# Ranked heads from tile 1 on, fp16 loads over GpSimd's ring, and reordering on VectorE, in a fused attention and MoE kernel

## The chip, the cores and the metric

The kernel runs on one core of one Trainium2 chip. The metric is the device time of one execution in microseconds. The kernel before takes 238.72 us (median of 3 runs, 238.43 to 239.06). The engines are TensorE (PE in the profile; PEld is its weight load), VectorE (DVE), ScalarE (ACT), GpSimd (POOL) and SyncE (SP), which here only issues DMAs.

## The reference

The input is causal attention over 4 batches, 8 heads, 768 positions and head size 64, followed by a MoE-like layer. Three of the eight heads ("retrieval") attend to all earlier positions; the others see 4 sink positions and a window of 64.

```python
scores = q @ k.T / sqrt(64)
mask   = causal if is_retrieval[h] else causal & (is_sink | in_window)
x      = softmax(where(mask, scores, -1e9)) @ v     # -> [3072, 512]
h      = x @ w_in                                   # w_in  [512, 2048]
out    = (h - tanh(h)) @ w_out                      # w_out [2048, 512]
```

## The kernel before

The work goes by tiles of 256 positions: 12 tiles, three to a batch. The attention of a tile is woven into the MoE matmuls of the tile before, so that TensorE always has something to do. A small planner written in Python orders the operations of each engine; a tile of MoE work is eight units, about 2.1 us each.

From tile 3 on the heads are handled "by rank": the position of each head among the retrieval and the other heads is held in registers, and streaming heads take a cheaper near path. The kernel before brings q, k and v as fp32 over SyncE's queue, and GpSimd copies each head to its rank and makes fp16 of it:

```python
def ranked(t):
    return first and fast and t >= NG          # NG = 3 tiles per batch
...
def cast_ranked(t):
    for half in range(2):
        for nm in ("qk", "v"):
            for rank in range(half * HH, half * HH + HH):
                at = bass.ds(regs["POOL"][rank], 1)
                ...
                nc.gpsimd.tensor_copy(
                    out=t16[t % 2][:, :, :, rank : rank + 1, :],
                    in_=raws["rqk", t][0]()[:, :, :, at, :],
                )
    for i in range(NB):                        # then q and k are transposed by DMA
        nc.sync.dma_start_transpose(out=qk[...], in_=t16[t % 2][:, i]...)
```

The attention output of a ranked tile (`x16t`) is also transposed by DMA into `xT`, which the first MoE matmuls (`ph`) of the next stretch need:

```python
def st_X_tile(t):
    for i in range(NB):
        nc.sync.dma_start_transpose(
            out=xTs[t]()[:, :, i * 128 : i * 128 + 128],
            in_=x16s[t]()[:, i, :, :].rearrange("p h d -> p (h d)"),
        )
```

How early a tile's attention is done before its MoE work is one constant, in units:

```python
AHEAD = 2.0
ahead = (AHEAD if t > NG else 0.0, AHEAD) if ranked(t) else (0.0, 0.0)
SPAN[t] = (lo + cut[t % NG] - ahead[0], lo + cut[t % NG + 1] - ahead[1])
```

The softmax here doesn't subtract the row's maximum and nothing guards it: scores larger than these inputs give would overflow.

Of the kernel before, what the change touches and what calls it, by code (L numbers as in the profile page):

```python
# [16 lines left out]
class Plan:  # L17
# [16 lines left out]
    def op(self, eng, ns, fn, r=(), w=(), dma=None, prio=None, port=False, after=None, behind=None):  # L34
        i = len(self.ops)
        deps = set() if after is None else {after}
        for k in r:
            if k in self.writer:
                deps.add(self.writer[k])
            if k[0] in self.PSUM:  # L40
                deps.update(j for j in self.readers.get(k, ()) if self.ops[j][0] != eng)
            self.readers.setdefault(k, []).append(i)
# [16 lines left out]
    def run(self):  # L59
# [45 lines left out]
        while len(order) < n:  # L105
# [28 lines left out]
            _, ns, _, _, dma, _, port, _ = self.ops[i]  # L134
            self.start[i] = t
# [4 lines left out]
            for u in followers[i]:  # L140
                ready[u] = max(ready[u], t + ns)
                left[u] -= 1
                if not left[u]:
                    enqueue(u)
            if dma:
                packets, each = dma
                rings["POOL" if e == "POOL" else "SP"].append(
                    [i, t + ns + (1200 if e == "POOL" else 300), each, packets * each / 16]
                )
            else:  # L150
                finish(i, t + ns + self.RESULT[e])
# [6 lines left out]
def kernel(  # L158
# [64 lines left out]
    gate = const.tile([1, 1], FP16, name="gate")  # L223
    A4 = const.tile([128, 4, 128], FP16, name="A4")
    sinks = const.tile([128, 128], FP16, name="sinks")
    nz = const.tile([128, 2 * H], FP32, name="nz")
# [30 lines left out]
    def program(first):  # L257

        P = Plan(bufs)
        op = P.op  # L260
        rot = {}
# [26 lines left out]
        def paired(nm, t):  # L288

            return nm != "v" and t == 0  # L290

        def load(t, names="qkv", halves=(None,), blocks=range(NB), after=None):

            b, g = divmod(t, NG)
            for half in halves:
                h0, nh = (0, H) if half is None else (half * HH, HH)
                for nm in names:
                    src = {"q": q, "k": k, "v": v}[nm]
                    tag = "rv" if nm == "v" else "rqk"
                    if (tag, t) not in raws:  # L300
                        idx = rot[tag] = rot.get(tag, -1) + 1
                        shape = [128, NB, H, D] if nm == "v" else [128, NB, 2, H, D]
                        raws[tag, t] = (
                            lazy(raw_pool, shape, FP32, tag, f"raw_{tag}{t}"), idx
                        )
                    if paired(nm, t):
                        op(
                            "SP", max(420, 128 * nh * 1.1),
                            lambda nm=nm, src=src, h0=h0, nh=nh: nc.sync.dma_start(
                                out=raw_pairs(nm, t)[:, h0 : h0 + nh, :, :].rearrange(  # L310
                                    "p h e d -> p h (e d)"
                                ),
                                in_=src[b, h0 : h0 + nh, g * TT : (g + 1) * TT, :].rearrange(
                                    "h (p e) d -> p h (e d)", e=NB
                                ),
                            ),
                            w=[
                                key for x in (range(2) if half is None else (half,))
                                for key in raw_keys(nm, t, x)
                            ],  # L320
                            dma=(128 * nh, 26.0), after=after,
                        )
                        continue
                    for i in blocks:
                        s0 = g * TT + i * 128
                        op(
                            "SP", max(420, 128 * nh * 1.1),
                            lambda nm=nm, i=i, src=src, s0=s0, h0=h0, nh=nh: nc.sync.dma_start(
                                out=raw_of(nm, t)[:, i, h0 : h0 + nh, :],
                                in_=src[b, h0 : h0 + nh, s0 : s0 + 128, :].rearrange("h p d -> p h d"),  # L330
                            ),
                            w=[
                                key for x in (range(2) if half is None else (half,))
                                for key in raw_keys(nm, t, x, (i,))
                            ],
                            dma=(128 * nh, 18.3), after=after,
                        )

        def raw_pairs(nm, t):
            r = raws["rqk", t][0]()  # L340
            return r[:].rearrange("p i x h d -> p (i x h d)").rearrange(
# [3 lines left out]
        def raw_of(nm, t):  # L345
            if paired(nm, t):
                return raw_pairs(nm, t).rearrange("p h e d -> p e h d")
            r = raws["rv" if nm == "v" else "rqk", t][0]()
            return r[:] if nm == "v" else r[:, :, "qk".index(nm), :, :]

        def raw_keys(nm, t, half, blocks=range(NB)):
            tag = "rv" if nm == "v" else "rqk"
            return [(tag, raws[tag, t][1], nm, half, i) for i in blocks]
# [11 lines left out]
        def load_cast(t, w_after=(), names="qkv"):  # L365

            b, g = divmod(t, NG)
            for nm in names:
# [21 lines left out]
                for i in range(NB):  # L390
                    behind(
                        930, lambda fn=fn, i=i: fn((i,)), r=w_after,
                        w=[key for half in range(2) for key in t16_keys(nm, t, half, (i,))],
                        dma=(128 * H, 18.5),
                    )

# [25 lines left out]


# [8 lines left out]
        for half in range(2):  # L432
            load(0, "qk", (half,))
            load(0, "v", (half,))
        if first:

            op("POOL", 204, lambda: nc.gpsimd.memset(ones[:], 1.0), w=["ones"])
# [6 lines left out]
            if fast:  # L444
# [10 lines left out]
            def select(m, src, fill, base, step, mult, key, cmp=ALU.is_ge):  # L455
# [8 lines left out]


            select(ident16[:], ones[:], 0.0, 0, 1, -1, "ident", ALU.is_equal)
            select(A4[:, 2, :], ones[:], 0.5, window_i - 1, -1, 1, "A4")
            select(sinks[:], ones[:], 0.5, n_sink_i - 1, 0, -1, "sinks")
            op(
                "DVE", 220,  # L470
                lambda: nc.vector.tensor_max(out=A4[:, 0, :], in0=A4[:, 2, :], in1=sinks[:]),
                r=["A4", "sinks"], w=["A40"],
            )
            select(A4[:, 2, :], A4[:, 2, :], 0.0, 0, 1, -1, "A4")
            select(A4[:, 3, :], ones[:], 0.5, -(128 - window_i + 1), -1, 1, "A43")
            op(
                "DVE", 220,
                lambda: nc.vector.tensor_max(out=A4[:, 1, :], in0=A4[:, 3, :], in1=sinks[:]),
                r=["A43", "sinks"], w=["A41"],
            )  # L480
            select(A4[:, 0, :], A4[:, 0, :], 0.0, 0, 1, -1, "A40")
            if fast:
                select(mS[0:64, 3, :], ones[0:64, :], 0.0, window_i - 65, -1, 1, "mS3")
                select(mS[64:128, 3, :], ones[64:128, :], 0.0, n_sink_i - 1, 0, -1, "mS3")

# [19 lines left out]
            def make_rflag0():  # L505

                nc.vector.scalar_tensor_tensor(
                    out=rflag0[:], in0=sinks[:, 0:1].to_broadcast([128, H]), scalar=0.75,
# [3 lines left out]
            op("DVE", 165, make_rflag0, r=["sinks", "rflag"], w=["rflag0"])  # L512

# [20 lines left out]
        def ranked(t):  # L534
            return first and fast and t >= NG

        def by_rank(after):

            def dve(ns, fn, r, w):
                op("DVE", ns, fn, r=r, w=w, after=after)  # L540
# [54 lines left out]
            )  # L595
            dve(
# [15 lines left out]
                    out=rflagr0[:], in0=sinks[:, 0:1].to_broadcast([128, NGEN]), scalar=0.75,  # L612
# [10 lines left out]
                r=["A4", "A40", "A41", "A43"], w=["mS"], port=True, after=after,  # L623
# [4 lines left out]
                r=["mS3"], w=["mS"], port=True, after=after,  # L628
            )
            for e, et in (("POOL", Engine.Pool), ("DVE", Engine.DVE)):  # L630

                def get(e=e, et=et):
                    regs[e] = nc.values_load_multi_w_load_instructions(
                        perm_i[0:1, :], engines=[et], min_val=0, max_val=H - 1,
                        skip_runtime_bounds_check_because="each head has one rank below H",
                    )[1]

                op(e, 900, get, r=["perm"], w=["regs" + e])
# [9 lines left out]
        def t16_keys(nm, t, half, blocks=range(NB)):  # L648
            return [("t16", t % 2, nm, half, i) for i in blocks]

        def cast_qk(t, engines, halves=range(2)):

            for half in halves:
                for nm, es in zip("qk", engines):
                    hs = slice(half * HH, half * HH + HH)
                    cast_op(
                        es[half], NB * HH * D,
                        lambda nm=nm, hs=hs: t16[t % 2][:, :, "qk".index(nm), hs, :],
                        lambda nm=nm, hs=hs: raw_of(nm, t)[:, :, hs, :],
                        r=raw_keys(nm, t, half), w=t16_keys(nm, t, half),  # L660
                    )

        def cast_ranked(t):
            b, g = divmod(t, NG)
            lo = g * NB
            if b not in v1s:
                ones_v(b)
            for half in range(2):
                for nm in ("qk", "v"):
                    for rank in range(half * HH, half * HH + HH):  # L670

# [771 lines left out]
```

## Time and profile before

| | before |
|---|---|
| time, median | 238.72 us |
| TensorE busy | 94% of the span |
| VectorE, GpSimd busy | 59%, 38% |
| first `ph` matmul | 18.93 us |
| last matmul ends | 231.81 us |
| TensorE work by weights | 205.2 us, so 26.6 us idle before the last matmul |

The work by weights counts each matmul at the distance at which the same kind follows itself undisturbed (109 ns for 256 columns, and so on; the prediction tells how). "Idle" below always means time up to the last matmul less this work.

The columns of these lines are packets, megabytes, and the time that the packets took as a share of the span of the 16 DMA engines; packets overlap, so the shares can add up to more than 100%. The last line is from another part of the page: issues, kilobytes of each, median us from issue to landing.

```profile
q1 hardware_dynamic: 92642, 28.98, 60.5%
q0 software_dynamic: 15168, 5.77, 20.7%
...
raw_rqk<-in_q_dram SPq DMA_DIRECT2D x20, 256.0 KB, 4.7
```

q1 is SyncE's queue, q0 is GpSimd's ring.

### The profile page before, as it was taken

The page shows a single profiled execution, that of the slowest core. Times are in us where ns is not written, and L with a number is a line of the kernel's source. Part 1 is how long each engine was busy: PE and PEld are TensorE (multiplying, and loading weights), DVE is VectorE, ACT ScalarE, POOL GpSimd, SP SyncE. Part 2 cuts the span into 40 slices and gives each one's busy share as a digit, 9 for nine tenths or more (in the row PEclk, how much of TensorE's full clock was granted, in tenths as well). Part 3 has the DMA queues.
Part 4 walks back from the last instruction along what each step waited for, and adds up shares of the span by engine and source line. Part 5 has one row for each costly group of instructions (what it writes and reads, how often), then busy time and mean ns, then how long its engine had stood idle before and what let it go on. Part 6 is the DMA issues. An engine that isn't in the chain of part 4 may idle for free. (4 is left out here: it accounts for less than half of the span.)

```text
span 236.7 us, 5895 instructions
## 1 busy us (share of the span) xinstructions
PE 221.5 (94%) x2220; PEld 157.8 (67%) x2220; DVE 139.0 (59%) x343; ACT 143.6 (61%) x221; POOL 90.5 (38%) x218
## 2 busy tenths in 40 slices
PE   0889899999999999999999999999999999999991
PEld 0346687756776777777676777776776777777661
DVE  1856665864488657767666655667766546443300
ACT  3668677884588387466686649537759464444320
POOL 5999420089818068480814904606300000000000
PEclk9999999999999999999999999999999999999999
DMA  5999999999997999979989695998712101310121
GB/s 128 209 140 172 204 181 204 197 228 224 206 225 182 151 248 184 227 153 206 239 168 214 136 186 130 186 171 179 134 47 66 38 31 47 90 38 9 44 89 51
DMA packets 108130, 35.29 MB, mean 149 GB/s; under 512 B 100290, under 2 KB 104642, under 8 KB 108098
## 3 DMA queue, kind: packets, MB, share of 16 engines
q1 hardware_dynamic: 92642, 28.98, 60.5%
q0 software_dynamic: 15168, 5.77, 20.7%
q8 instruction: 18, 0.29, 0.5%
q10 hardware_dynamic: 288, 0.14, 0.2%
q14 instruction: 14, 0.11, 0.2%
HBM read 27.27 MB, written 6.29 MB: 142 GB/s over the span
## 5 line engine op out<-in xcount | busy, mean ns | idle before, releaser
L1135 PE MATMUL ph<-xT,win 128*128 128x256 f16 x768 | 101.7, 273 | 0.6 <-DMA win<-in_moe_w_in_dram 0.3
L1194 PE MATMUL po<-wout,gt 128*128 128x512 f16 (+1 forms) x400 | 98.0, 371 | 0.3 <-ACT ot L1170 0.3
L1148 ACT ACTIVATE th<-ph 128x512 f32<-128x512 f32 x96 | 57.6, 601 | 59.6 <-PE ph L1135 58.2
L1155 DVE SCALAR_TENSOR_TENSOR gt<-th,ph 128x512 f16<-128x512 f32 x96 | 65.4, 684 | 44.9 <-ACT th L1148 44.4
L1135 PEld LDWEIGHTS <-win 128*128 128x128 f16 x768 | 80.0, 114 | 13.0 <-issue 1.9
L961 ACT ACTIVATE pt<-sc 128x1024 f16<-128x1024 f32 (+1 forms) x78 | 68.5, 926 | 11.4 <-PE sc L941 10.9
L1194 PEld LDWEIGHTS <-gt 128*128 128x128 f16 x400 | 36.4, 98 | 24.6 <-issue 0.9
L680 POOL CAST t<-raw_rqk 128x256 f16 x72 | 28.5, 440 | 63.3 <-DMA raw_rqk<-in_k_dram 48.1
L1030 PEld LDWEIGHTS <-pt 128*128 128x128 f16 x552 | 25.9, 98 | 10.4 <-issue 0.9
L1030 PE MATMUL av<-v,pt 128*128 128x65 f16 x304 | 26.0, 195 | 0.1
L941 PE MATMUL sc<-qk 64*128 64x128 f16 (+1 forms) x412 | 23.8, 240 | 1.7 <-DVE qk L826 1.7
L941 PEld LDWEIGHTS <-qk 64*128 64x128 f16 x412 | 13.7, 94 | 13.5 <-issue 8.9
L675 POOL CAST v<-raw_rv 128x128 f16 x72 | 21.1, 335 | 4.2 <-DMA raw_rv<-in_v_dram 4.2
L1060 DVE TENSOR_TENSOR x16t<-av,rinv 128x128 f32 x72 | 20.8, 289 | 2.3 <-DVE rinv L1050 0.3
L1030 PE MATMUL av<-vf,pt 128*128 128x65 f16 x248 | 19.6, 193 | 0.0
L1170 ACT ACTIVATE ot<-po 128x512 f32<-128x512 f32 (+1 forms) x24 | 14.3, 596 | 8.5 <-PE po L1194 8.4
L996 DVE TENSOR_TENSOR pt<-pt,m 128x1024 f16<-128x1024 f16 x16 | 12.3, 768 | 8.0 <-ACT pt L961 8.0
L1050 DVE RECIPROCAL rinv<-av 128x4 f32<-128x4 f32 x48 | 8.6, 179 | 13.4 <-PE av L1030 13.4
L986 DVE TENSOR_TENSOR pt<-pt,mS 128x512 f16<-128x512 f16 x24 | 9.8, 449 | 6.7 <-ACT pt L961 6.7
L843 PEld LDWEIGHTS <-t 128*128 128x128 f16 x48 | 3.9, 107 | 8.9 <-ACT t L644 6.8
L523 DVE TENSOR_SCALAR m<-A,thr 128x512 f16<-128x512 f16 x16 | 7.4, 501 | 1.7 <-PE sc L928 1.2
L751 POOL TENSOR_TENSOR vf<-v,rflagr 128x260 f16<-128x260 f16 x12 | 7.5, 634 | 0.0
(95 smaller groups left out, 90.8 us busy)
## 6 DMA issues: line engine op xcount, KB each, us to landing
out_dram<-ot SPq DMA_DIRECT2D x23, 256.0 KB, 2.3
raw_rqk<-in_q_dram SPq DMA_DIRECT2D x20, 256.0 KB, 4.7
raw_rqk<-in_k_dram SPq DMA_DIRECT2D x20, 256.0 KB, 4.5
raw_rv<-in_v_dram SPq DMA_DIRECT2D x18, 256.0 KB, 4.4
win<-in_moe_w_in_dram POOLq DMA_DIRECT2D x4, 512.0 KB, 8.8
wout<-in_moe_w_out_dram POOLq DMA_DIRECT2D x4, 512.0 KB, 12.4
raw_rv<-in_v_dram SPq DMA_DIRECT2D x4, 128.0 KB, 4.7
t<-in_q_dram POOLq DMA_DIRECT2D x4, 128.0 KB, 9.5
```

The source lines that it names most:

```text
L675: nc.gpsimd.tensor_copy(out=v1s[b]()[:, lo : lo + NB, rank : rank + 1, 0:D], in_=raw_of("v", t)[:, :, at, :],)
L680: nc.gpsimd.tensor_copy(out=t16[t % 2][:, :, :, rank : rank + 1, :], in_=raws["rqk", t][0]()[:, :, :, at, :],)
L941: nc.tensor.matmul(out=sc()[:, hh, o : o + nb * 128].rearrange("p (i c) -> p i c", c=128), lhsT=ks.rearrange("p i c -> p (i c)")[p_, jb * ...
L961: lambda pt=pt, gi=gi, wid=wid, sc=sc: nc.scalar.activation(out=pt()[:, :, 512 * gi : 512 * gi + wid], in_=sc()[:, :, 0:wid], func=AF.Exp, ...
L996: nc.vector.tensor_mul(out=pv, in0=pv, in1=m4[:, h0 : h0 + 2, 256:512].unsqueeze(2).to_broadcast([128, 2, 2, 256]),)
L1030: nc.tensor.matmul(out=av()[:, i, hh, :], lhsT=pt()[:, hh, co : co + 128], rhs=vv, start=(jb == first_jb), stop=(jb == qb),)
L1060: nc.vector.tensor_mul(out=x16s[t]()[:, :, at, :], in0=av()[:, :, hh : hh + 1, 0:D], in1=rinv()[:, :, hh : hh + 1].unsqueeze(3).to_broadca ...
L1135: nc.tensor.matmul(out=ph()[:, j, :], lhsT=w()[:, cb, c0 + fb % 4 : c0 + 512 : 4], rhs=xTs[t]()[:, cb, :], start=(cb == 0), stop=(cb == HP ...
L1148: lambda: nc.scalar.activation(out=th()[:], in_=ph()[:], func=AF.Tanh, scale=1.0 / XS),
L1155: lambda: nc.vector.scalar_tensor_tensor(out=gts[t]()[:, u * FU : (u + 1) * FU, :], in0=th()[:], scalar=-XS, in1=ph()[:], op0=ALU.mult, op ...
L1170: nc.scalar.activation(out=ot()[:, c0:c1], in_=po()[:, c0:c1], func=AF.Copy, scale=1.0 / XS)
L1194: nc.tensor.matmul(out=po()[:, c0:c1], lhsT=gts[t]()[:, f, ts * 128 : ts * 128 + 128], rhs=w_out_t[f // 4]()[:, f % 4, c0:c1], start=(f == ...
```

## The change

The intent: (1) handle batch 0 by rank from tile 1 on, so that TensorE loses mask matmuls, scores and attention matmuls; (2) bring q, k and v as fp16, converted by the DMA itself on GpSimd's ring, in the order of heads (all but k of tile 0); (3) let VectorE put the heads in the order of ranks, from fp16 to fp16, so that GpSimd has no casts left. The core of the diff, cut:

```diff
         def ranked(t):
-            return first and fast and t >= NG
+            return by_ranks and t > 0
...
+        def load_flight(t, nm, pairs=range(HP), blocks=range(NB), after=None):
+            ...
+            for i in blocks:
+                behind(
+                    200 + 128 * nh * 0.72,
+                    lambda i=i, s0=s0: nc.gpsimd.dma_start(       # fp32 in memory -> fp16 in SBUF
+                        out=raw_of(nm, t)[:, i, h0 : h0 + nh, :],
+                        in_=src[b, h0 : h0 + nh, s0 : s0 + 128, :].rearrange("h p d -> p h d"),
+                    ), ...
+                )
...
         def cast_ranked(t):
-                            at = bass.ds(regs["POOL"][rank], 1)
-                                nc.gpsimd.tensor_copy(
+            es = ('DVE',) if t == 1 else ('DVE',) if t == 2 else ('DVE',)
+                        cast_rank(t, nm, rank, es[rank % len(es)])
...
-            ahead = (AHEAD if t > NG else 0.0, AHEAD) if ranked(t) else (0.0, 0.0)
+            ahead = (AHEAD, AHEAD) if ranked(t) else (0.0, 0.0)
```

The rest rewrites the start: q and v of tile 0 are loaded over the ring, its k still as fp32 over SyncE's queue, the rank arithmetic comes first, the masks are made on VectorE, tiles 1 and 2 are transposed by TensorE and tile 1's x as well.

## The prediction

> **What bounds the kernel now.** I read the page first, for the busy shares.
>
> ```profile
> span 236.7 us, 5895 instructions
> PE 221.5 (94%) x2220; PEld 157.8 (67%) x2220; DVE 139.0 (59%) x343; ACT 143.6 (61%) x221; POOL 90.5 (38%) x218
> PE   0889899999999999999999999999999999999991
> DVE  1856665864488657767666655667766546443300
> POOL 5999420089818068480814904606300000000000
> ```
>
> TensorE is busy from slice 2 to the end; nothing else comes near. VectorE and GpSimd have room on average. Next the waits of TensorE.
>
> ```profile
> PE tp0q L843 <- ACT t L644: 6.0, 1, 6.0
> PE sc L941 <- DVE qk L826: 1.7, 3, 0.7
> PE xp L1108 <- DVE x L1074: 1.1, 3, 0.6
> ```
>
> After the first 6.0 us the recorded waits are about 5 us in all. That flatters the kernel, because "busy" covers the latency of a matmul. So I took the distance between the starts of consecutive matmuls from the trace (median): 109 ns for 256 columns, 216 for 512, 29 for a 65-column attention-times-v, 56 for a 128-column transpose. Score matmuls use half of the rows and two run side by side: 28 for 128 columns, 56 for 256. These weights times the counts give 205.2 us of TensorE work. The last matmul ends at 231.8, so 26.6 us are idle by this measure. The timeline tells where:
>
> ```profile
> 6.00 0.39 PE L843 MATMUL tp0q<-ident,t 128*128 128x128 f16 x2 [6.00 <-ACT t L644]
> ...
> 18.93 1.06 PE L1135 MATMUL ph<-xT,win 128*128 128x256 f16 x8
> ```
>
> Until the first MoE matmul at 18.93 only 5.5 us of work are done: 13.5 us idle in the start-up of tile 0, a chain of short operations over four engines. From 18.9 to 60 us another 5 us or so are idle, and from 60 us on only 0.3 to 0.6 us per 10 us. So there are two places to gain: less TensorE work, worth its full size after 60 us, and a shorter start-up. Relief for GpSimd by itself is worth nothing.
>
> ```profile
> L680 POOL CAST t<-raw_rqk 128x256 f16 x72 | 28.5, 440 | 63.3 <-DMA raw_rqk<-in_k_dram 48.1
> L675 POOL CAST v<-raw_rv 128x128 f16 x72 | 21.1, 335 | 4.2 <-DMA raw_rv<-in_v_dram 4.2
> L1155 DVE SCALAR_TENSOR_TENSOR gt<-th,ph 128x512 f16<-128x512 f32 x96 | 65.4, 684 | 44.9 <-ACT th L1148 44.4
> L928 PE MATMUL sc<-m,ident 128*128 128x512 f16 x8 | 2.5, 400 | 0.0
> ```
>
> The first two groups are the copies by rank that go from GpSimd to VectorE; the third is what VectorE must not delay, as it frees the bank that the next MoE matmuls write; the fourth disappears.
>
> **What the Trainium skill says.** "DMA: Bandwidth & Descriptors", section "SWDGE vs HWDGE vs iDMA": a DMA that changes the type must be issued from GpSimd, whose cores write the descriptors into rings in SBUF. The trace agrees that GpSimd pays for it: the 12 such issues for q, k, v took 0.87 to 1.10 us each. "SBUF — State Buffer", section "Who interferes with whom": a VectorE copy in a two-port mode and GpSimd hold a shared port exclusively, and the later one blocks. The trace agrees:
>
> ```profile
> 5.82 1.73 DVE L523 TENSOR_SCALAR m<-A,thr 128x512 f16<-128x512 f16 x4 [0.44 <-POOL A L458]
> ...
> 6.09 1.98 POOL L378 DMA_DIRECT2D t<-in_q_dram  x2
> ```
>
> Four mask operations beside two DMA issues took 1.73 us; the third of them alone is 815 ns in the trace, until its DMA issue was over, while the undisturbed ones are 335 ns. "VectorE: DVE Perf Modes", section "What auto-detection actually checks": copies of 16-bit data within SBUF take the fastest mode. Here the one such copy (128x128) took 184 ns, and the next operation started 119 ns after it. So a copy by rank should fall from GpSimd's 440 and 335 ns to about 0.17 us (256 elements) and 0.12 us (128) of VectorE's queue, an estimate. The register operation in front of each runs ahead in the sequencer (57 ns).
>
> **The change, part by part.** The order of instructions of both kernels gives exact counts for the path that runs.
> 1. Tiles 1 and 2 by rank, half of their heads with the near path. Mask matmuls 8 x 512 columns go: 8 x 216 ns = 1.7 us. Scores: 24 fewer of 256 columns, 8 more of 128: 24 x 56 - 8 x 28 = 1.1 us. Attention-times-v: 552 to 512, 40 x 29 ns = 1.2 us. Transposes: 8 more for k of tile 0 (once by head, again by rank), 8 fewer for x of tile 2, which goes by DMA: zero. Total 4.0 us less TensorE work, 201.2 us. Of it about 0.4 us lay before 18.9 us.
> 2. GpSimd: 144 casts (50 us) go; 66 DMA issues of 0.93 us (61 us) plus four half ones come instead of 12. It stays at some 40% and off the path. SP loses its loads. Bytes read from memory are the same; the written ones halve. In steady state the loads are two tiles ahead, and six issues are 5.6 us of a tile's 17 us: hidden.
> 3. VectorE: 88 qk copies and 88 v copies plus 16 for tile 0: 88 x 0.17 + 104 x 0.12 = 27 us, some 2.5 us per tile. Without overlaps it now spends about 10 us of a 17 us tile (8 x 0.60 for gt, 8 x 0.28 for x, four masks 2.8, reciprocals 0.4), so it goes from 60% to 75%. TensorE has two banks for ph, so a delay of about 2 us is hidden. I allow 1 us of new waits in all.
> 4. Start-up. ACT loses casts (three of 0.62 us become two), and the masks come from VectorE before the data lands. But the rank arithmetic, which lay at 41 to 46 us beside MoE work, moves into the first 13 us, with the register load (845 ns in the trace), four more masks, 16 copies, four more strided copies of k (0.34) and the xT copies that ACT did (0.2). The first MoE matmul needs the fourth xT, and before it VectorE's order has, from 5.15 us when thr is ready: 12 masks at 0.42, as disturbed as now (5.0); 20 small operations (2.2); the load (0.85); eight strided copies at 0.34 (2.7); x and reciprocals (2.0); xT and tr10 (1.0); 16 copies of tile 0 (1.9); eight of tile 1 (1.4). Together 17.1, so the first ph at about 22 us if nothing overlaps, and 20.0 if the masks are undisturbed (0.26). I take 21.2, that is 2.3 us later than 18.93.
>
> **The sum.** Before: 18.93 + 199.75 us of remaining work + 13.1 idle = 231.8. After: 5.1 us of work lie before the first ph, 196.1 remain. 21.2 + 196.1 + 13.1 + 1.0 = 231.4; the tail to the end of the span is 4.9 and the measured time is 2.0 above the span: 238.3. Against this stands that the idle time between 18.9 and 60 us (5 us) should shrink: tile 1 has no mask matmuls in front of its scores and fewer exponentials (ACT's count falls by two of 1.02 us and four of 0.81 us), GpSimd no longer makes 1.07 us products that block VectorE's masks, and its SBUF-reading casts are gone, which brings pt masks from 768 to about 690 ns. I give that 2.0 us: 236.3 us.
>
> **Rivals.** (a) The start-up is not delayed: transposes and ACT, not VectorE, set it, and q arrives without a cast; then the whole 4.0 us and the 2.0 us show: about 233 us. For it: VectorE had 2.2 us busy of the 5 us from 10 to 15 us. Against: 17 us of work stand in its queue now. (b) VectorE becomes the bound in tile 0's MoE phase: 14.7 us of its work (eight gt, masks, x, copies for tiles 1 and 2) face about 12.4 us of TensorE work there. Then another 2 to 3 us are lost and it is 239 to 241 us. (c) Descriptor writing and fast copies block each other in every tile: 16 copies per tile, a fifth of them held 0.3 us is 1 us of VectorE per tile, hidden at 75%; if it is 3 us per tile, the occupancy passes 90% and TensorE waits: 242 us and more. (d) The single ring delivers too late: a landing took 4 to 5 us quiet and up to 13.7 us behind weights. Tile 2 sits between weights on the ring, so a wait at 35 to 45 us is possible: 1 to 3 us.
>
> **Range and chances.** 236.3 us, a little below the before. (a) gives the low end near 232, (b) and (d) the high end near 240.5. Faster by over 2% means under 233.9: 0.27, since it needs the start-up to cost nothing. Slower by over 2% means over 243.5: 0.04, needing (c).
>
> **What would show it.** Step 1: the counts of matmuls above, and TensorE from 60 us to the end as dense as now. Step 2: no casts on GpSimd, about 70 issues near 0.93 us. Step 3: copies of 150 to 250 ns with means raised by collisions, VectorE near 70% busy. Step 4: the first ph matmul at 20 to 22 us. I am wrong if it comes at or before 19 us, if TensorE waits for gt by more than a few us in the later tiles, or if the copies take over 300 ns.

## More of the kernel before

The view of the tile xT ends with the time from issue to landing of the DMA transposes of x:

```profile
DMA to landing us min/median/max: 2.3/2.8/4.7
```

## The result, and the profile after

The changed kernel takes 255.2 us (median of 4 runs, 251.41 to 255.41) against 238.8 us for the kernel before in the same rounds. Ratios here are the mean time of one kernel's fast runs over that of the other's of the same rounds, so they are not quite the ratio of the medians quoted. Executions over 1.5% slower than the fastest of the same kernel are left out of the means. The ratio is 1.0605, with a 95% interval of 1.0474 to 1.0737: slower by 6%. Two of its four runs (255.38 and 255.41) differ by only 0.1% from the profiled one (255.03); the other run is 251.41. So the changed kernel itself scatters by 4 us, where the kernel before scattered by 0.6 in these rounds.

The page of the changed kernel, busy shares and slices:

```profile
span 253.3 us, 5884 instructions
...
PE 224.8 (89%) x2156; PEld 157.7 (62%) x2156; DVE 164.8 (65%) x552; ACT 135.9 (54%) x209; POOL 93.8 (37%) x132
...
PE   0868989798889999995999999993999999999992
...
DVE  6999688484988876864668747754577555543410
...
PEclk9999999999999999998899999999799999999998
```

Against the rows of before: TensorE was 9 or 8 throughout. Now there are two holes, a 5 and a 3, in slices 19 and 28 (a slice is 6.3 us), and the row of the granted clock dips at or just after them. VectorE is at 65%, so it is not full. The waits of TensorE (total us, times, longest):

```profile
PE ph L1409 <- DMA xT<-x16t: 7.6, 2, 4.4
PE sc L1172 <- DVE m L706: 5.9, 2, 5.5
PE xp L1382 <- DVE x L1324: 2.0, 1, 2.0
PE av L1275 <- POOL vf L981: 1.5, 1, 1.5
```

The first line did not exist before. The first MoE matmuls of two tiles wait for the DMA transpose of x. The timeline shows the end of the start-up, and the first of the two waits:

```profile
22.05 2.77 PE L1409 MATMUL ph<-xT,win 128*128 128x256 f16 x12
...
114.85 0.34 PE L1275 MATMUL av<-v,pt 128*128 128x65 f16 x6
118.35 2.55 PE L1409 MATMUL ph<-xT,win 128*128 128x256 f16 x12 [3.15 <-DMA xT<-x16t]
```

And SyncE's part of the same timeline, the two transposes that were waited for:

```profile
109.77 2.56 SPq L1362 DMA_TRANSPOSE xT<-x16t  x2
```

They were issued at 109.77 and 111.05 us. TensorE ran out of other work at 115.19. By the trace's records they landed at 116.04 and 118.30, that is after 6.3 and 7.2 us. With the 2.8 us that such a transpose took in the median before, the second would have landed at 113.85 and nothing would have waited. At the second place (tile 8) they took 7.9 and 8.6 us. Over the whole kernel the view of xT says:

```profile
DMA to landing us min/median/max: 2.4/3.9/8.6
```

What shares the DMA engines with them is in the queue table and among the issues:

```profile
q0 software_dynamic: 75520, 13.37, 72.6%
q1 hardware_dynamic: 34400, 14.03, 28.2%
...
raw_rqk<-in_q_dram POOLq DMA_DIRECT2D x22, 128.0 KB, 6.0
```

All loads of q, k and v moved from q1 to q0, except that of tile 0's k. They write half the bytes, yet a load lands in 6.0 us, not 4.7. The packets fit this: in the trace a converting packet (128 bytes written) took 32 ns in the median in both kernels, a plain 256-byte packet of SyncE's loads 18 ns. The number of packets per load is the same, so by these medians the load holds the engines longer although it writes less. The kernel before already had 12,288 of the converting packets, so this could be read there.

The wait brings a second loss. In windows of 1 us (columns: window, length, busy time and instructions of PE, PEld, DVE, ACT and POOL, then the granted clock, the DMA share, GB/s):

```profile
117.00:118.00 1.00, 0.00 (x0) 0.00 (x0) 0.21 (x2) 0.00 (x0) 0.00 (x0) 1.00 3.10 146
118.00:119.00 1.00, 0.65 (x5) 0.53 (x6) 1.00 (x6) 0.00 (x0) 0.00 (x0) 0.81 3.20 150
119.00:120.00 1.00, 1.00 (x6) 0.74 (x5) 0.56 (x5) 0.00 (x0) 0.00 (x0) 0.50 2.74 173
...
121.00:122.00 1.00, 1.00 (x5) 0.41 (x4) 0.67 (x3) 0.00 (x0) 0.00 (x0) 0.50 0.00 0
122.00:123.00 1.00, 1.00 (x12) 0.62 (x12) 0.37 (x2) 0.00 (x0) 0.00 (x0) 0.99 0.09 18
```

After the wait TensorE ran at half its clock for over 3 us: 5 or 6 matmuls per us, then 12. The Trainium skill's page "TensorE: Matmul & The Clock Gate", section "What's actually happening", describes this: the clock is throttled to one half after an idle window of some 3.4 us and released after a busy one. The trace agrees in kind and in the length of the slow stretch: its clock records give one half from 118.62 to 122.03 us, and again from 176.6 to 180 us after the second wait. The idle time before the first was a little shorter than the page's window, 3.15 us, and other runs had the half clock after still shorter gaps (last section).

The start hides the same loss. In the timeline above, the twelve `ph` matmuls from 22.05 us took 2.77 us; at 109 ns each and the latency of the last they should take about half of that. From there up to 26.46 us matmuls of one kind follow each other at twice their normal distance. The trace has no clock record before 26.46 us, and the first one says full clock; the PEclk row prints 9 also where there is no record. So TensorE still ran at half clock there: from 22.05 to 26.46 us it did 2.25 us of work by weights, and lost 2.2 us. In the kernel before, the first record of full clock is at 14.95 us, ahead of its first `ph`. In all twelve profiled runs with the new start-up TensorE was at half clock until 23.6 to 26.6 us; five of them have it in their records, beginning at 16.7 to 18.0 us. In the four runs with the old start-up it was at full clock from 16.0 us at the latest. One of the five, e_start, shows the dip in its row:

```profile
PEclk9986999799999999999799999999799999999999
```

The share of each part in the 16.5 us by which the last matmul ends later (248.28 less 231.81), with idle as defined above:

| | before | after | difference |
|---|---|---|---|
| TensorE work | 205.2 | 201.2 | -4.0 |
| idle, 0 to 40 us | 17.1 | 22.6 | +5.4 |
| idle, 40 to 80 us | 3.9 | 6.6 | +2.6 |
| idle, 80 us to the last matmul | 5.5 | 18.0 | +12.4 |

The 4.0 us that the change was made for are there. Of the 20.4 us that ate them, 12.4 are after 80 us, where before only 5.5 were idle. They hold 7.6 us of waits for xT, and 3.3 us that the slow matmuls after these waits took beyond their normal distance (1.7 at 115 to 125 us, 1.6 at 175 to 185 us). The two make 10.9 of the 12.4 us. The 5.4 us before 40 us are 3.4 before the first `ph` and 2.0 after it (from 3.65 to 5.64 us), and these 2.0 are the half clock up to 26.46 us.

### The profile page after: what moved, and what is told of

It is laid out like the page before. It is cut to its first block, busy times and chain, and to the rows that moved or that the text cites. A ratio compares the mean times of both kernels' runs of the same rounds, so it can differ in the third digit from the quotient of the medians.

```text
span 253.3 us, 5884 instructions
## 1 busy us (share of the span) xinstructions
PE 224.8 (89%) x2156; PEld 157.7 (62%) x2156; DVE 164.8 (65%) x552; ACT 135.9 (54%) x209; POOL 93.8 (37%) x132
## 5 line engine op out<-in xcount | busy, mean ns | idle before, releaser
L1409 PE MATMUL ph<-xT,win 128*128 128x256 f16 x768 | 105.5, 279 | 9.1 <-DMA xT<-x16t 7.6
L1205 ACT ACTIVATE pt<-sc 128x1024 f16<-128x1024 f32 (+1 forms) x72 | 63.3, 930 | 19.8 <-PE sc L1185 19.7
L1275 PEld LDWEIGHTS <-pt 128*128 128x128 f16 x512 | 25.1, 100 | 15.2 <-issue 4.7
L961 POOL TENSOR_TENSOR vf<-v,rflagr 128x260 f16<-128x260 f16 x16 | 10.7, 684 | 44.3 <-DVE v L1026 44.2
L1310 DVE TENSOR_TENSOR x16t<-av,rinv 128x128 f32 x88 | 25.3, 288 | 2.2 <-DVE rinv L1300 0.4
L433 POOL DMA_DIRECT2D raw_rqk<-in_q_dram x26 | 22.9, 889 | 5.4 <-DVE qk L1026 2.7
L1185 PE MATMUL sc<-qk 64*128 64x128 f16 (+1 forms) x396 | 22.2, 242 | 1.5 <-DMA qk<-t 1.0
L1275 PE MATMUL av<-vf,pt 128*128 128x65 f16 x224 | 18.7, 193 | 2.8 <-POOL vf L981 1.5
L1185 PEld LDWEIGHTS <-qk 64*128 64x128 f16 x396 | 13.3, 96 | 11.7 <-issue 9.9
L433 POOL DMA_DIRECT2D raw_rqk<-in_k_dram x22 | 19.6, 897 | 1.6 <-DMA wout<-in_moe_w_out_dram 1.6
L433 POOL DMA_DIRECT2D raw_rv<-in_v_dram x22 | 19.5, 901 | 1.5 <-DMA wout<-in_moe_w_out_dram 1.5
L1026 DVE COPY t<-raw_rqk 128x256 f16 x88 | 15.2, 244 | 7.3 <-DMA raw_rqk<-in_k_dram 5.1
L981 POOL COPY vf<-v 64x260 f16<-64x260 f16 (+1 forms) x12 | 5.9, 489 | 34.7 <-DVE v L1026 34.3
L1300 DVE RECIPROCAL rinv<-av 128x4 f32<-128x4 f32 x48 | 8.5, 177 | 13.4 <-PE av L1275 13.2
L1230 DVE TENSOR_TENSOR pt<-pt,mS 128x512 f16<-128x512 f16 x32 | 12.1, 418 | 7.4 <-ACT pt L1205 7.4
```

Source lines behind the costliest of these rows:

```text
L433: lambda i=i, s0=s0: nc.gpsimd.dma_start(out=raw_of(nm, t)[:, i, h0 : h0 + nh, :], in_=src[b, h0 : h0 + nh, s0 : s0 + 128, :].rearrange("h ...
L1026: engs[e].tensor_copy(out=dst, in_=src)
L1185: nc.tensor.matmul(out=sc()[:, hh, o : o + nb * 128].rearrange("p (i c) -> p i c", c=128), lhsT=ks.rearrange("p i c -> p (i c)")[p_, jb * ...
L1205: lambda pt=pt, gi=gi, wid=wid, sc=sc: nc.scalar.activation(out=pt()[:, :, 512 * gi : 512 * gi + wid], in_=sc()[:, :, 0:wid], func=AF.Exp, ...
L1230: nc.vector.tensor_mul(out=pv, in0=pv, in1=m[:, 384:640].unsqueeze(1).to_broadcast([128, 2, 256]),)
L1275: nc.tensor.matmul(out=av()[:, i, hh, :], lhsT=pt()[:, hh, co : co + 128], rhs=vv, start=(jb == first_jb), stop=(jb == qb),)
```

## The experiments

Fourteen kernels ran, all with correct results; medians of before in their rounds were 238.4 to 239.0. The main theory, called R (for ring): loads on the ring lengthen the DMA transposes of x, and the slack of two units is then too small. The rivals: VectorE is too loaded with the copies (V; the first expectations call it D), and the start-up and tiles 1 and 2 by rank are what costs (S). The table is for reference; "changed" and "before" name the kernel edited.

| run | edited | median us | ratio | idle 0-40 / 40-80 / 80-end | waits for xT |
|---|---|---|---|---|---|
| kernel before | | 238.8 | 1 | 17.1 / 3.9 / 5.5 | 0 |
| changed kernel | | 255.2 | 1.0605 | 22.6 / 6.6 / 18.0 | 7.6 |
| e_sp_pool | changed | 257.4 | 1.0741 | 25.8 / 15.9 / 7.4 | 0 |
| e_sp_dve | changed | 264.0 | 1.1023 | 26.5 / 16.9 / 11.7 | 2.0 |
| e_ring_only | before | 248.9 | 1.0386 | 17.1 / 6.1 / 10.7 | 2.9 |
| e_xt_pe | changed | 249.1 | 1.0385 | 23.2 / 5.9 / 9.0 | 0 |
| e_sp_gated | changed | 249.6 | 1.0422 | 22.8 / 4.9 / 13.2 | 3.7 |
| e_ring_pool | before | 243.5 | 1.0159 | 17.1 / 6.7 / 7.3 | 2.4 |
| e_ahead4 | changed | 244.4 | 1.0177 | 22.8 / 6.9 / 6.8 | 0 |
| e_start | changed | 258.5 | 1.0751 | 22.1 / 9.5 / 18.7 | 8.4 |
| e_before_ahead4 | before | 240.6 | 1.0075 | 17.1 / 3.9 / 7.3 | 0 |
| e_gated_ahead4 | changed | 245.9 | 1.0281 | 22.8 / 4.7 / 9.8 | 0 |
| e_pool_ahead4 | changed | 244.5 | 1.0197 | 22.8 / 6.4 / 10.5 (slow run) | 0.2 |
| e_v_act | changed | 246.2 | 1.0338 | 24.1 / 5.3 / 7.0 | 0 |
| e_vf_act | changed | 245.9 | 1.0203 | 24.3 / 7.5 / 7.2 (slow run) | 0 |
| e_both_act | changed | 241.9 | 1.0110 | 21.8 / 5.4 / 7.1 | 0 |

The idle columns are of the one profiled run, the medians of all runs.

### Loads back to SyncE: e_sp_pool and e_sp_dve

```diff
         def flown(t):
-            return first and fast and t in range(0,NTT)
+            return first and fast and t in range(0,NG)     # from tile 3 on: fp32 on SyncE
# e_sp_pool alone, GpSimd for the copies from tile 3 on:
-            es = ('DVE',) if t == 1 else ('DVE',) if t == 2 else ('DVE',)
+            es = ('DVE',) if t < NG else ('POOL',)
```

> Batch 0 stays by rank with the new start-up, but from tile 3 on the loads are fp32 on SyncE's queue and GpSimd casts by rank, as before. Theory R (the loads on GpSimd's ring crowd the DMA transposes; TensorE waits 3.3 and 4.6 us for xT and then runs at half clock for a while): xT lands within 5 us, no wait of TensorE for xT over 1 us, 241 to 246 us. Rival S (the start-up and tiles 1 and 2 by rank are what costs): stays at 249 us or more. Rival D (VectorE's copies delay everything): cannot be told from R here, 241 to 246 us.

> As e_sp_pool, but VectorE makes the rank copies, from fp32. R: loads share the queue of the transposes, xT lands within 5 us, 241 to 247 us though VectorE works some 30 us more than in e_sp_pool. D: stays at 249 us or more, with waits of TensorE for gt or for xT because x16t is late. S: 249 us or more.

Measured: 257.39 us (257.25 to 257.62) and 263.96 us (263.39 to 264.75). Both lie above all ranges that R gave. They are spoiled in total by a flaw of the edit: nothing holds tile 3's loads back, so on SyncE's queue they ran beside the weights and tile 2. Some 10 us of idle time came between 40 and 80 us, part of it half clock (in e_sp_pool recorded from 38.5 to 45.3 and from 59.0 to 65.8 us). From the first `ph` of tile 3 to the last matmul, which leaves that out, the stretch is 155.5 us for e_sp_pool, against 153.1 before and 169.1 in the changed kernel. e_sp_pool has no wait for xT, whose transposes land in at most 4.8 us. e_sp_dve (158.5 us for the stretch) has one of 2.0 us, behind transposes that landed in 6.6 and 5.3 us, though no ring load had run since 57 us. So the ring is not the only thing that lengthens them; what did it there is not known. In all this speaks for R, but not cleanly; hence the gated kernel below.

### The reverse, ring loads alone: e_ring_only and e_ring_pool

The kernel before, with fp16 ring loads from tile 3 on, tiles 0 to 2 untouched:

```diff
+        def ringed(t):
+            return first and fast and t >= NG
...
+                        if ringed(t):
+                            behind(200 + 128 * nh * 0.72,
+                                lambda ...: nc.gpsimd.dma_start(out=raw_of(nm, t)[:, i], in_=...), ...)
+                            continue
# e_ring_only also (e_ring_pool leaves the copies on GpSimd):
-                            at = bass.ds(regs["POOL"][rank], 1)
-                                nc.gpsimd.tensor_copy(
+                            at = bass.ds(regs["DVE"][rank], 1)
+                                nc.vector.tensor_copy(
```

> The kernel before with its start-up and batch 0 by heads; only from tile 3 on the loads come as fp16 over GpSimd's ring and VectorE copies by rank. R: xT lands in 6 us or more at times, TensorE waits for it some us, 243 to 250 us. S: 237 to 240 us. D: 243 to 250 us too, but with xT landing in under 5 us after its issue and the issue late.

> The kernel before, with the loads from tile 3 on as fp16 over GpSimd's ring, but GpSimd goes on making the copies by rank. R (ring against transposes): like e_ring_only, 245 to 250 us, with transposes that take 5 to 8 us. Rival D (VectorE's copies are what costs in e_ring_only): 238 to 241 us.

Measured: e_ring_only 248.87 us (245.92 to 249.48), e_ring_pool 243.51 us (242.67 to 247.18, the highest one slow; the median of its fast runs is 242.72). So the ring loads by themselves, with an untouched start and the copies left on GpSimd, cost about 3.9 us on the old schedule. That lies between what R (245 to 250) and its rival (238 to 241) expected, and the ratio of 1.0159 (1.0036 to 1.0282) is not far clear of 1. The same wait appears, 2.4 us in two pieces: 1.6 us before tile 3, whose second transpose landed in 6.5 us, and 0.8 us before tile 5, whose transposes landed in 4.2 and 3.9 us but went out only 2.7 us after x16t was ready. Moving the copies to VectorE costs a further 6.2 us on that schedule (fast runs, with 239.0 and 238.9 us for the kernel before), and TensorE then waits 2.0 us for gt, against 0.3 in e_ring_pool. So R is confirmed in direction; V has a part too, unless more slack hides it.

### x transposed by TensorE: e_xt_pe

```diff
         def st_X_tile(t):
-            if t in (1,):
+            if True:                       # all tiles: TensorE transposes x, no DMA
```

> The changed kernel with x of every tile transposed by TensorE instead of DMA: 72 transposes more at 56 ns are 4.0 us more TensorE work. R: the two waits (7.9 us) and the slow clock after them (some 3 us) go, so 246 to 249 us, unless qk's transposes are late as well. S or D: 257 to 260 us, the added work on top.

Measured: 249.07 us (248.61 to 250.37). The idle time after 80 us falls from 18.0 to 9.0 us, at a price of 4.5 us of added TensorE work (201.2 to 205.7; 80 transposes, not the 72 expected), and the waits for xT are gone. The total is at the upper edge of what R expected. With 9.0 of the 12.4 us gone, these waits, not the loads' own arrival, were most of the late loss.

### SyncE loads done properly: e_sp_gated

e_sp_pool plus a gate that holds tile 3's loads until tile 2's k has landed.

```diff
+        def gate_tile_3():
+            gated[0] = op("SP", 400, fn, r=raw_keys("k", 2), w=["gate"], dma=(1, 20.0))
...
-                            after=None if t == 1 else first_S[t * HP + hp],
+                            after=gated[0] if t == 1 else first_S[t * HP + hp],
```

> e_sp_pool again, with the loads of tile 3 held back until tile 2's k has landed, which the kernel before also did: without it they took the DMA engines from the weights and tile 2 between 20 and 65 us. Theory R (the ring loads delay the transposes; the start-up costs some 3 us and the saved TensorE work pays for it): 238 to 243 us, first MoE matmul still at 22 us, from the first MoE matmul of tile 3 to the end within 3 us of the 153 us of before. Rival S (batch 0 by rank itself costs most): 248 us or more.

Measured: 249.62 us (248.83 to 250.64). Better than the changed kernel by 5.6 us, but not back. By its number it falls in the range of rival S (248 or more), and R's (238 to 243, with the late stretch within 3 us of before) is missed: that stretch is 158.7 us against 153.1. Against the kernel before 5.7 us of idle time came before 40 us and 7.7 after 80, so the start is a part, but not most. After 80 us one wait for xT of 3.7 us is left, with half clock after it from 118.2 to 121.6 us. Yet here the transposes land in 2.7 us in the median. SyncE's own waits from 95 to 118 us tell why:

```profile
SPq L891 <- POOL v L1026: 5.5, 1, 5.5
```

L891 is the transpose of q and k of a later tile. It stood at the head of SyncE's queue until GpSimd had made its copies by rank (GpSimd itself had waited 5.7 us for a load of k, until 104.6 us), and what came behind it had to be worked off afterwards, in order:

```profile
108.07 1.27 SPq L891 DMA_TRANSPOSE qk<-t  x1
109.39 1.42 SPq L329 DMA_DIRECT2D raw_rqk<-in_q_dram  x2
110.92 1.50 SPq L1456 DMA_DIRECT2D out_dram<-ot  x1
112.47 1.36 SPq L891 DMA_TRANSPOSE qk<-t  x1
113.94 2.52 SPq L1362 DMA_TRANSPOSE xT<-x16t  x2
```

VectorE had finished x16t at 108.65 us, but its transposes went out at 113.94 and 115.2. So the same wait came from a late issue, not from a slow transfer. Both are a lack of slack.

### More slack: e_ahead4, and its control e_before_ahead4

```diff
-        AHEAD = 2.0
+        AHEAD = 4.0
```

> The changed kernel with the attention of a tile planned two units (some 4 us) earlier against the MoE that needs it (AHEAD 4 instead of 2). R: the transposes take as long as ever, but the two waits for xT, 3.3 and 4.6 us, mostly fit into the added slack: 243 to 249 us, granted clock above 0.99. Rival T (TensorE waits because the transposes cannot pass the loads at all, so they come later in proportion; or VectorE is the limit): 252 us or more.

> The kernel before with AHEAD 4 in place of 2: the control for the gain of 10.8 us that AHEAD 4 brought to the changed kernel. Theory R (the ring loads lengthen the transposes of x, and only there the two slots of slack are too few): the transposes of x of the kernel before land in 2.8 us and TensorE does not wait for them, so nothing is to be won: 238 to 240.5 us. Rival (AHEAD 2 is too short for any kernel, and the change only inherited it): it gains here too, 230 to 236 us.

Measured: the changed kernel falls from 255.2 to 244.41 us (242.99 to 244.63), ratio 1.0177. The kernel before rises to 240.63 us (240.35 to 241.25), ratio 1.0075 with an interval from 1.0041. So the slack is worth nothing to the kernel before, whose transposes are quick, and 10.8 us to the changed one. (The granted clock was 0.997 in the profiled run, as expected, but 0.973 to 0.981 in the other three, which took no longer.) The view of xT in e_ahead4 shows that the transfers did not get quick:

```profile
DMA to landing us min/median/max: 2.4/4.0/7.1
```

They still take up to 7.1 us, but TensorE's list of waits has no line for xT any more. The two that were late before land 1.2 us (tile 5) and 2.5 us (tile 8) before their use; the tightest is now tile 3's, by 0.14 us. The idle time after 80 us is 6.8 us, so 11.2 of the 12.4 us extra are gone with this one constant.

In the kernel before the same margins can be read from the trace: the transposes of tile 5 landed at 109.88 us and were used at 110.05. A spare of 0.17 us was all there was.

### Slack with other places for loads and copies: e_gated_ahead4 and e_pool_ahead4

```diff
# e_gated_ahead4: e_sp_gated with AHEAD 4
# e_pool_ahead4: the changed kernel with AHEAD 4 and
-            es = ('DVE',) if t == 1 else ('DVE',) if t == 2 else ('DVE',)
+            es = ('DVE',) if t < NG else ('POOL',)
```

> The changed kernel with fp32 loads on SyncE's queue and GpSimd's copies from tile 3 on, held by the gate (249.6 us), and AHEAD 4. Its one wait for a transpose of x (3.7 us) came of a late issue: SyncE's queue stood 5.5 us at the transpose of q and k, which waited for GpSimd's copies by rank, and the transposes of x stood behind it. Theory R with head-of-line blocking: two more slots take that wait away with the slow clock that followed it: 243 to 246 us, with no wait for xT over 1 us. Rival (what the loads on SyncE lose is the bandwidth of fp32 loads beside the weights of the start, before tile 3): 248 to 250 us.

> The changed kernel with the ring loads kept, but GpSimd for the copies by rank from tile 3 on, and AHEAD 4 (which alone gave 244.4 us). Theory V (VectorE's 65% load still delays x16t, masks and evictions: moving the copies was worth 5.4 us between the two ring experiments on the kernel before): 239 to 242 us. Theory R alone (with four slots of slack the place of the copies no longer matters): 243.5 to 245.5 us. If GpSimd, with loads to issue and copies of up to 430 ns, becomes late itself: over 246 us, with waits for copies of GpSimd in TensorE's list.

Measured: e_gated_ahead4 245.92 us (244.71 to 246.59), without the wait for xT, inside what R expected. e_pool_ahead4 244.51 us (242.96 to 247.75, the highest one slow; 244.2 without it), the same as e_ahead4's 244.41: with four units of slack it does not matter whether VectorE or GpSimd does the copies. So the 6.2 us of the ring experiments (5.4 in the expectation, with the slow run) are no independent cost of VectorE's load. The reading that fits both is that slow copies make x16t, and with it the transposes, late, which the slack hides; that link itself no run isolates.

### The start: e_start, e_v_act, e_vf_act, e_both_act

```diff
# e_start: the changed kernel, x of tile 0 copied by ScalarE, and four masks later
-                    st_X(n, "o", "DVE")
+                    st_X(n, "o", "ACT")
# e_v_act: AHEAD 4; the eight rank copies of tile 0's v on ScalarE
-                at = bass.ds(regs["DVE"][rank], 1)
+                at = bass.ds(regs["ACT" if nm == "v" else "DVE"][rank], 1)
# e_vf_act: AHEAD 4; the copy of v into vf on ScalarE for tiles 0 to 2
-                "POOL", 60 + 260 * (j1 - j0),
+                "ACT" if t < NG else "POOL", 60 + 260 * (j1 - j0),
# e_both_act: e_v_act and e_vf_act together
```

> The changed kernel with some load taken from VectorE in the start-up: ACT copies x of tile 0 out of PSUM again, and the four masks of the ranks come later in the order. If VectorE's queue sets the first MoE matmul: it moves from 22.05 to about 21 us and the whole gains 0.5 to 1.5 us. If the transposes or the DMA set it: 22 us as before. The waits for xT at 115 and 172 us stay, so 252 to 255 us either way.

> The changed kernel with AHEAD 4 (244.4 us) and the 8 rank copies of tile 0's v on ScalarE, which is idle from 14.4 to 17.5 us. Theory B (the 16 rank copies of tile 0, 13.3 to 15.8 us of VectorE, stand before x and so before the transposes of x and the first matmul with the first weights): TensorE's gap of 2 us before xp shrinks to 0.7 to 1.2 us, the first ph goes from 22.25 to 21.0 to 21.5 us, the total to 243 to 243.8 us. Rival (the start is bound by the arrival of q, k and v of tiles 1 and 2 over the ring): first ph stays at 22.0 to 22.4 us and the total at 244.4.

> The changed kernel with AHEAD 4 (244.4 us), where the copy of v into the upper blocks of vf is on ScalarE for the first three tiles, not on GpSimd, where it stands between ring issues of 0.9 us. Theory I (issues delay GpSimd's other work): the wait of TensorE for vf, 2.1 us at 48 us, goes, and 242 to 243 us come out. Rival (the wait is for v itself, which arrives late over the ring, or the next wait takes its place at once): the total stays within 0.7 us of 244.4.

> Both of the two edits together with AHEAD 4. If theories B and I hold, their gains add up, as they lie at different times: 241 to 242.5 us, still above the kernel before (238.8). If either is hidden behind the arrival of the ring loads: 243.5 to 245 us.

Measured: e_start 258.51 us (255.78 to 258.94), above the 252 to 255 expected; its first `ph` is at 22.27 us, not earlier. It is no clean test: the records have half clock from 16.7 to 23.6 us and, after a wait of 2.7 us for vf, from 47.5 to 50.9 us. e_v_act 246.18 us (244.62 to 248.06), in neither range: the wait of 1.9 us before xp shrinks to 0.6 (0.7 to 1.2 expected), yet the first `ph` comes at 22.51 us. The timeline of VectorE in e_v_act shows the next wait in its place:

```profile
16.61 1.96 DVE L1026 COPY t<-raw_rqk 128x256 f16 x6 [0.82 <-DMA raw_rqk<-in_k_dram]
```

These are the rank copies of tile 1, which wait for its k from the ring, and their transposes stand ahead of the first `ph` in TensorE's order. So theory B fell: the block of copies of tile 0 is one of several things that end near 22 us, and removing it uncovers the next. In all four profiled runs of this group the first `ph` stays at 22.2 to 22.5 us, and in all four TensorE was at half clock there, so none tells when it would come at full clock.

e_vf_act is inconclusive: two of its four runs are slow, and the fast ones are 242.32 and 244.85 us. Its wait for vf is gone from the list. e_both_act gave 241.94 us (240.21 to 242.42), ratio 1.0110 with an interval of 1.0054 to 1.0165: the best form of the changed kernel, as expected for the pair, but its parts do not add up, since e_v_act alone was no gain. Its idle time falls by 1.0 us before 40 us and by 1.5 us from 40 to 80 us against e_ahead4. For the first of these the clock is enough: its first record of full clock is at 23.7 us, against 26.2 in e_ahead4, and 2.5 us at half clock are some 1.2 us of work. e_v_act's profiled run lost its clock once more, from 34.1 to 40.9 us. No run beats the kernel before, so none replaces it.

## Why the prediction was wrong

The prediction was 236.3 us with a range of 232.0 to 240.5; 255.2 came out. It went point by point:

- **Step 1, right.** TensorE's work fell to 201.2 us, exactly as counted. The gain is real, it is just not all that happened.
- **Step 2, half right, and here is the step that failed.** "No casts on GpSimd, about 70 issues near 0.93 us" holds:

```profile
L433 POOL DMA_DIRECT2D raw_rqk<-in_q_dram x26 | 22.9, 889 | 5.4 <-DVE qk L1026 2.7
...
L433 POOL DMA_DIRECT2D raw_rqk<-in_k_dram x22 | 19.6, 897 | 1.6 <-DMA wout<-in_moe_w_out_dram 1.6
L433 POOL DMA_DIRECT2D raw_rv<-in_v_dram x22 | 19.5, 901 | 1.5 <-DMA wout<-in_moe_w_out_dram 1.5
```

  The sentence that failed is "In steady state the loads are two tiles ahead, and six issues are 5.6 us of a tile's 17 us: hidden." It asked whether GpSimd has the time to issue, and whether the loads themselves come in time. Past the start both were so. It did not ask what the loads do to others on the same DMA engines. The Trainium skill's page "DMA: Bandwidth & Descriptors", section "Issuing engines are not separate DMA queues", says that DMAs of all engines end up on the same 16 DMA engines and interleave; the trace agrees, with transposes of x at up to 8.6 us beside the ring loads, against 4.7 before, and 6.1 to 6.7 when only the ring loads were added (e_ring_only, e_ring_pool). Rival (d), "the single ring delivers too late", looked at tile 2 only and at arrivals only.
- **Step 3, right in size, wrong in the allowance.** The copies of q and k took 244 ns in the mean and 15.2 us together, which is the foretold 0.17 us of the queue each; those of v took 13.4 us for 88, 0.15 us each against 0.12. VectorE is 65% busy, a little under what was foretold:

```profile
L1026 DVE COPY t<-raw_rqk 128x256 f16 x88 | 15.2, 244 | 7.3 <-DMA raw_rqk<-in_k_dram 5.1
...
L1429 DVE SCALAR_TENSOR_TENSOR gt<-th,ph 128x512 f16<-128x512 f32 x96 | 65.2, 682 | 37.4 <-ACT th L1422 37.2
```

  TensorE waited for gt for only 1.2 us. Rivals (b) and (c) did not come. But the allowance of "1 us of new waits in all" was far too small: after 80 us alone 12.4 us of idle time were added, because the waits were for DMA transposes, which the allowance had not asked about.
- **Step 4, nearly right.** The first `ph` was foretold for 21.2 us, within 20 to 22; it came at 22.05, at the upper edge. That it came about there for the reason given is not shown: the experiments on VectorE's queue did not move it, and TensorE's half clock before it, which the step does not have, is a second candidate. Among the figures that it rests on, one of the masks called undisturbed (336 ns, at 6.21 us) ran inside a DMA issue of GpSimd.
- **The sum.** The 2.0 us credited for fewer idle gaps between 18.9 and 60 us were wrong in sign. From the first `ph` to 80 us the changed kernel lost, where the prediction gained. The prediction has the last matmul at 229.4 us (231.4 less 2.0), so the miss to 248.28 is 18.9 us: 0.8 for the first `ph`, about 12.4 for the idle time after 80 us, and the remaining 5.7 for the stretch between. Of these, 2.2 are the half clock up to 26.46 us, which the credit did not ask about. Two readings were loose but do not change the sum: the recorded waits after the first 6.0 us are 4.1 us, not about 5, and the idle time from 18.93 to 60 us is 6.1 us, not 5.
- **What could have been read before.** Two numbers of the kernel before pointed at it: the spare time of 0.17 us with which tile 5's xT landed, and 32 against 18 ns per packet for the converting loads that it already had.

What stays open. Why TensorE reaches its full clock at 26.46 us and not at 14.95 was not tested. From 15 us to the first `ph` it did 1.9 us of work by weights; at half clock this takes 1.9 us more, so the clock may also be a part of the 3.1 us by which the first `ph` is late, but no run shows it. For most of the 2.6 us from 40 to 80 us no cause was found. A rival for the length of the two long landings is in the trace as well: beside instruction fetches of 16 KB at 112.9 and 169.7 us the DMA engines nearly stopped, at 9 GB/s from 113.5 to 114.5 us and at 7 to 11 GB/s from 170.0 to 171.5 us, inside these landings. The kernel before has such a stretch too (15 to 28 GB/s from 91.5 to 93.0 us), with no transpose of x under way. The ring can lengthen a transpose without one: in e_ahead4 one took 7.0 us (107.94 to 114.94) while the rate never fell under 118 GB/s. How much of the 8.6 us is the standstill's was not tested. And why single kernels of this family scatter by 3 to 5 us is open. The kernel before is not free of it: in one call its fast runs went from 238.59 to 241.47 us.

## What to carry to other kernels

When a load is moved to another queue, ask for each DMA that shares the 16 DMA engines how long before its use it lands, and what it is worth if it lands twice as late; a transfer that lands 0.2 us before its use is on the critical path already. Half the bytes is no relief when the packets are as many and each takes longer. To see the clock, compare the distance of like matmuls with their usual one: here a busy TensorE with no clock record ran at half speed for 4.4 us. When a schedule constant was tuned with one set of transfers, tune it again with the other before judging the change: here one constant was 10.8 of 16.4 us.

## What the Trainium skill lacked or had wrong

- "DMA: Bandwidth & Descriptors" says that a converting DMA must go over GpSimd, but gives no cost of the transfer itself. Here a converting packet (256 bytes read, 128 written) took 32 ns in the median, a plain 256-byte one 18 ns.
- The same page says that DMAs of all issuers interleave, but not what a short DMA transpose loses beside ring loads: 2.8 us in the median and at most 4.7 before, 3.9 and 8.6 after.
- "TensorE: Matmul & The Clock Gate" gives an idle window of about 3.4 us before the clock falls. Here an idle gap of 3.15 us was enough for a half clock of 3.41 us, and in e_sp_dve one of 1.99 us (before 132.55 us; half clock from 133.6 to 137.1), while one of 2.11 us in e_ring_only (before 168.49 us) had none after it. The half clock began after work had resumed (0.81 in the window from 118 to 119 us, 0.50 after).
- No page gives a figure for what stands behind a DMA that waits at the head of its issuer's queue: a transpose that waited at the head of SyncE's queue held finished x16t back by 5.3 us in e_sp_gated (108.65 to 113.94 us).
